# First tile's queries and keys in two transfers, and products of zeros on TensorE ahead of the first tile: a windowed-attention and mixture kernel on one core

## The chip, the core and the metric

The kernel runs on one core of a Trainium2 chip. The core has five engines with a queue each, taken in order: TensorE (PE in the profile; its weight loads are PEld), VectorE (DVE), ScalarE (ACT), GpSimd (POOL) and SyncE (SP, which issues the transfers here). They meet only at semaphores. The metric is the device time of one execution in microseconds (us); several executions are timed, and their median counts.

## The reference

There are 8 batches, 8 heads, 576 positions and 64 numbers per head. Each position attends to itself and the 63 before it. The result, 4608 tokens of 512 numbers, goes through a dense layer of 1024 with a softmax-weighted activation and a layer norm, and through a second dense layer back to 512.

```python
rel = pos[:, None] - pos[None, :]
mask = (rel >= 0) & (rel < window)            # window = 64
scores = np.where(mask, scale * (q @ k.T), -1e9)
attn = exp(scores - max) / (sum + 1e-9)
x = attn @ v                                   # tokens x 512
...
h = x @ w_in                                   # 512 -> 1024
solu = h * softmax(h)
ln = (solu - mean) / sqrt(var + 1e-6) * g_ln
y = ln @ w_out                                 # 1024 -> 512
```

## The kernel before, in words

The 4608 tokens are cut into 36 tiles of 128 (two windows of 64). Per tile t the work runs through these steps; the names are those of the rows further down.

- `load`: one transfer brings the tile's queries and keys, `qk` (640 KB, 128 partitions by 1280 numbers, for four pairs of heads), a second one the values `v`. SP issues them.
- `scores` (L356): 16 products of 64x128 on PE into `pS`, in two plan steps x = 0 and 1 of eight products (two pairs of heads each). `pS` has one buffer, of two banks of the accumulation memory; the even heads lie in one, the odd heads in the other.
- `softmax`: eight masked row maxima on DVE (L371, a custom instruction and a read of its result `nmx`), eight exponentials on ACT (L376), the sums' reciprocals (`rec`, L389 and L392, DVE) and eight scalings (L394, on DVE for tile 0, on POOL for the others).
- `transposes` (L410, PE into `t`, copied out as `PT` by L415) and `values` (L434, PE into `pX`, copied out as `xH` by L444).
- `moe_in` (into `pH`, one buffer): plain products for tiles 0 to 2 (L466), for the later ones three passes of split operands (L477). `moe_norm`: row maximum on DVE (L492), exponential on ACT (L494), product with the row on DVE (L497, the last reader of `pH`), square sum (L503) and small steps.
- `moe_transpose` (L534) and `moe_out` (into `pO`: L559 for tile 0, L571 later) follow two tiles behind.

The weights come as 64-bit numbers in eight blocks: `w_0` to `w_3` of the first matrix, `w_4` to `w_7` of the second; `w_0` comes in two halves. Each block is turned into 32-bit numbers by one step on ACT (L278) and four on DVE, L280, L282, L284 and L286, which must follow each other. All of that falls into the first 62 us.

The order in each engine's queue is not the order of the code. `Plan` collects every step as an operation with an engine, a cost and the tiles that it reads and writes; `Plan.order` then lists them with its own clock: whichever operation can begin first by the listed costs goes next, and among those ready the one that is due first. PE's and SP's operations keep the program's order among themselves, except those marked `loose` (here `scores`, `transposes` and `values` of tile 0), which go when they are ready. A transfer is ready, by the plan's cost, 2600 ns after its issue. What is written into the queue in this order is then run strictly in it.

Of the kernel before, what the change touches and what calls it, by code (L numbers as in the profile page):

```python
# [11 lines left out]
BF16 = mybir.dt.bfloat16  # L12
# [5 lines left out]
P = 128  # L18
WIN = 64
# [138 lines left out]
def tile_window_attention_solu_moe(  # L158
# [17 lines left out]
    nc = tc.nc  # L176

    NT, DM = out.shape
    w_in, w_out = w_in.bitcast(I32), w_out.bitcast(I32)
    DFF = w_in.shape[1] // 2  # L180
    NPAIR = DM // P
# [8 lines left out]
    const = ctx.enter_context(tc.tile_pool(name="const", bufs=1))  # L190
# [6 lines left out]
    ps_o = ctx.enter_context(tc.tile_pool(name="ps_o", bufs=1, space=bass.MemoryType.PSUM))  # L197
# [15 lines left out]
    for first in (0, None, 1):  # L213
        t = masks[first] = const.tile([P, P], F32, name=f"mask{first}")
        nc.gpsimd.tensor_copy(t[:WIN], band[:WIN, :P])
        nc.gpsimd.tensor_copy(t[WIN:], band[WIN:, WIN:])
        if first is not None:
            nc.gpsimd.memset(t[first * WIN:(first + 1) * WIN, :WIN], NEG)

    w_inH = const.tile([P, NC, DFF], F32R, name="w_inH")  # L220
    w_outH = const.tile([P, NF, DM], F32R, name="w_outH")
    g_sb = const.tile([P, NF], F32, name="g_sb")
# [3 lines left out]
    plan = Plan(RINGS)  # L226

    def T(tag, n, shape, dtype=F32, pool=None):

        if (tag, n) not in plan.tiles:  # L230
            plan.tiles[tag, n] = (pool or sb).tile(
                shape, dtype, tag=tag, name=f"{tag}_{n}", bufs=RINGS[tag])
        return plan.tiles[tag, n]

    def first_of(t):

        return {0: 0, NBLK - 1: 1}.get(2 * t % NBLK)
# [56 lines left out]
    def prep(i):  # L294
        if i < NC:
            weight_block(i, w_in[i * P:(i + 1) * P, :].rearrange("p (a n) -> p a n", a=2), None)
        else:
            f = 2 * (i - NC)
            weight_block(i, w_out[f * P:(f + 2) * P, :].rearrange("(a p) n -> p a n", p=P),
                         lambda x: g_sb[:, f + x:f + x + 1])  # L300
# [10 lines left out]


    def QK(t):
        return T("qk", t, [P, NPAIR * (2 * P + WIN)])

    def Q(t):
        return QK(t)[:, :NPAIR * P].rearrange("d (p s) -> d p s", p=NPAIR)

    def K(t):
        return QK(t)[:, NPAIR * P:].rearrange("d (p s) -> d p s", p=NPAIR)  # L320

    def V(t, half):
        return T("v", t, [P, 2, DM])[:, half]
# [1 line left out]
    def load(t, parts=range(2)):  # L325

        if 0 in parts:
            plan.dma(P * P * 40, lambda: nc.sync.dma_start(QK(t), qk[t]), [], [("qk", t)])


        if 1 in parts:
            plan.dma(P * P * 32, lambda: nc.sync.dma_start(
                T("v", t, [P, 2, DM]).rearrange("p a n -> p (a n)"), v[t]), [], [("v", t)])

    def SS(t):
        return T("sS", t, [P, H, P])

    def PS(t):
        return T("pS", t, [P, 2, NPAIR, P], pool=ps_s)

    def scores(t):
        first = first_of(t)

        def emit(ps=range(NPAIR)):
            q, k = Q(t), K(t)

            for p in ps:
                for half in range(2):
                    for r in range(2):
                        rs = slice(r * D, (r + 1) * D)  # L350
                        keys = k[rs, p, half * WIN:half * WIN + P]
                        if first == half:
                            a = k[rs, p, (half + 1) * WIN:(half + 2) * WIN]
                            keys = bass.AP(
                                tensor=a.tensor, offset=a.offset, ap=[a.ap[0], [0, 2], a.ap[1]])
                        nc.tensor.matmul(  # L356
                            PS(t)[half * WIN:(half + 1) * WIN, r, p],
                            q[rs, p, half * WIN:(half + 1) * WIN], keys, start=True, stop=True)

        for x in range(2):  # L360
            plan.op("PE", 500, lambda x=x: emit((2 * x, 2 * x + 1)), [("qk", t)], [("pS", t, x)],
                    loose=t < LOOSE)

    def softmax(t):
        def cols(tag, h):
            return T(tag, t, [P, H], pool=st)[:, h:h + 1]

        mk = masks[first_of(t)]
        for h in range(H):

            plan.op("DVE", 215, lambda h=h: nc.vector.tensor_tensor_reduce(  # L371
                SS(t)[:, h], PS(t)[:, h % 2, h // 2], mk, scale=-SCALE, scalar=BIG,
                op0=ALU.add, op1=ALU.min, accum_out=cols("nmx", h)),
                [("pS", t, h // 4)], [("sS", t, h), ("nmx", t, h)], lat=300)
        for h in range(H):
            plan.op("ACT", 390, lambda h=h: nc.scalar.activation(  # L376
                SS(t)[:, h], SS(t)[:, h], AF.Exp, bias=cols("nmx", h), scale=-1.0,
                accum_out=cols("sm", h)),
                [("nmx", t, h)], [("sS", t, h), ("sm", t, h)], lat=400)

        def rec():
            return T("rec", t, [P, H], pool=st)

        engine, v, cost = ("POOL", nc.gpsimd, 360) if t else ("DVE", nc.vector, 200)
        n = H if t else H // 2
        for o in range(0, H, n):
            s = slice(o, o + n)
            R = ("rec", t, o)
            plan.op("DVE", 160, lambda s=s: nc.vector.tensor_scalar_add(  # L389
                rec()[:, s], T("sm", t, [P, H], pool=st)[:, s], 1e-9),  # L390
                [("sm", t, h) for h in range(o, o + n)], [R])
            plan.op("DVE", 160, lambda s=s: nc.vector.reciprocal(rec()[:, s], rec()[:, s]), [], [R])  # L392
            for h in range(o, o + n):
                plan.op(engine, cost, lambda h=h: v.tensor_scalar(  # L394
                    SS(t)[:, h], SS(t)[:, h], rec()[:, h:h + 1], 0.0, ALU.mult, ALU.add),
                    [R], [("sS", t, h)])
# [152 lines left out]
    def moe_out(t, middle=None):  # L549
# [25 lines left out]
        def ot():  # L575
            return T("ot", t, [P, DM])

        plan.op("ACT", 580, lambda: nc.scalar.copy(ot(), PO()), [tag], [("ot", t)])
        plan.dma(P * DM * 4, lambda: nc.sync.dma_start(out[t * P:(t + 1) * P, :], ot()), [("ot", t)], [])

    def on(f, t, *args):
        if 0 <= t < NTILE:
            f(t, *args)


    load(0, range(1))
    prep(0)
    scores(0)
    softmax(0)
    load(0, range(1, 2))  # L590
    prep(1)
    prep(2)
    load(1)
    transposes(0)
    values(0)
    scores(1)
    softmax(1)
    prep(3)
# [6 lines left out]
    prep(7)  # L605
    for t in range(NTILE + BEHIND):
        on(load, t + AHEAD + 1)
        if t == PLAIN_IN:
            for i in range(NC):
                split(i)  # L610
        on(moe_in, t, 0)
        if t == 0:
            scores(2)
            softmax(2)
# [70 lines left out]
```

## Time and profile before

| | |
|---|---|
| timed runs before | median 587.1 us of 3 (587.02 to 589.51) |
| the profiled execution, its own time | 586.37 us |
| its span, first to last instruction | 584.6 us |
| PE busy | 561.5 us, 96% of the span |
| DVE, ACT, POOL busy | 54%, 55%, 31% of the span |
| SP's transfers | 60.30 MB on one queue |

The span is shorter than the execution's own time by 1.8 us, which lie around it. PE is the busiest engine by far, but in the first tenth of the span, where the weights are turned into 32-bit numbers, DVE and ACT are the busy ones; later shares of one engine say nothing on that stretch.

### The profile page before, as it was taken

What the parts mean: (1) busy time and instruction counts of PE and PEld (TensorE: products, weight loads), DVE (VectorE), ACT (ScalarE), POOL (GpSimd) and SP (SyncE); (2) the same over time, 40 slices, a digit from 0 to 9 for tenths busy, and PEclk for the clock granted to TensorE, in tenths of its full rate; (3) what the DMA queues carried; (4) which work ended last, traced back from release to release, by engine and by line L of the source; (5) the groups of instructions that cost most, each with busy time, mean ns of one, the idle gap of its engine ahead of it and who ended that gap; (6) DMA issues with size and microseconds to landing.
All of it is one profiled execution on the core that took longest, in us unless ns stands there. A gap on an engine that the chain in (4) does not pass through costs nothing.

```text
span 584.6 us, 12281 instructions
## 1 busy us (share of the span) xinstructions
PE 561.5 (96%) x4576; PEld 449.3 (77%) x4576; DVE 316.5 (54%) x1171; ACT 320.7 (55%) x939; POOL 178.5 (31%) x406
## 2 busy tenths in 40 slices
PE   2788999999999999999999999999999999999997
PEld 2344688888888888888888888888888888888875
DVE  4879975555555554444455444555555555554330
ACT  4579975555555555555555555555555555553331
POOL 2034445322222333333333333333223222223110
PEclk9999999999999999999999999999999999999999
DMA  8972222222223223332222322322222222300001
GB/s 331 410 286 81 98 84 88 91 87 91 100 100 100 100 100 100 100 99 94 78 92 100 100 100 100 101 100 100 96 84 87 90 83 97 100 20 19 18 19 54
DMA packets 17562, 61.07 MB, mean 104 GB/s; under 512 B 2016, under 2 KB 2016, under 8 KB 17120
## 3 DMA queue, kind: packets, MB, share of 16 engines
q1 hardware_dynamic: 17504, 60.30, 29.5%
q8 instruction: 36, 0.59, 0.4%
q14 instruction: 22, 0.18, 0.1%
HBM read 50.86 MB, written 9.44 MB: 103 GB/s over the span
## 4 chain that ended last, share of the span: by engine, by line
PE 91%; DVE 4%; ACT 3%; DMA 1%; issue 0%; ACTq 0%; DVEq 0%
PE pO L571 34%; PE pH L477 32%; PE pX L434 6%; PE pS L356 6%; PE t L534 5%; PE t L410 5%; ACT sS L376 1%; PE pO L559 1%; DVE w L284 1%; PE pX L571 1%; PE pH L466 1%; DMA qk<-qk 1%; DVE w L280 1%; ACT w L278 1%; DVE mst L492 1%; DVE w L282 0%
## 5 line engine op out<-in xcount | busy, mean ns | idle before, releaser
L394 POOL TENSOR_SCALAR sS<-sS,rec 128x128 f32<-128x128 f32 x280 | 100.0, 379 | 340.8 <-DVE rec L392 325.1
L376 ACT ACTIVATE sS<-sS,nmx 128x128 f32<-128x128 f32 x288 | 112.3, 393 | 45.2 <-DVE nmx L371 45.2
L571 PE MATMUL pO<-w_outH,yH 128*128 128x512 f32 x272 | 111.6, 410 | 0.2 <-ACT yH L543 0.2
L571 PE MATMUL pO<-w,yH 128*128 128x512 f32 x272 | 108.0, 397 | 0.0
L477 PE MATMUL pH<-w_inH,xH 128*128 128x512 f32 x264 | 107.7, 408 | 0.0
L571 PE MATMUL pO<-w_outH,yL 128*128 128x512 f32 x272 | 107.0, 393 | 0.1
L477 PE MATMUL pH<-w_inH,xL 128*128 128x512 f32 x264 | 103.7, 393 | 0.0
L477 PE MATMUL pH<-w,xH 128*128 128x512 f32 x264 | 103.4, 395 | 0.0
L543 ACT CAST yH<-t 128x512 fp32r<-128x512 f32 x70 | 37.5, 588 | 103.4 <-PE t L534 103.4
L492 DVE TENSOR_REDUCE mst<-pH 128x1 f32<-128x1024 f32 x36 | 44.1, 1225 | 72.7 <-PE pH L477 70.7
L415 ACT COPY PT<-t 128x512 f32<-128x512 f32 x39 | 22.7, 587 | 83.4 <-PE t L410 83.4
L571 PEld LDWEIGHTS pO<-w_outH,yH 128*128 128x128 f32 x272 | 51.0, 187 | 17.1 <-issue 5.0
L571 PEld LDWEIGHTS pO<-w_outH,yL 128*128 128x128 f32 x272 | 51.1, 188 | 13.2 <-DVE yL L545 0.5
L514 POOL TENSOR_SCALAR e<-e,mst 128x512 f32<-128x512 f32 x72 | 55.5, 777 | 18.8 <-PE t L410 11.3
L477 PEld LDWEIGHTS pH<-w_inH,xL 128*128 128x128 f32 x264 | 49.6, 188 | 12.3 <-issue 0.2
L371 DVE CUSTOM_DVE_ANT_0 sS<-pS,maskNone 128x128 f32<-128x128 f32 x224 | 51.5, 286 | 13.9 <-PE pS L356 13.9
L571 PEld LDWEIGHTS pO<-w,yH 128*128 128x128 f32 x272 | 51.1, 188 | 10.2
L477 PEld LDWEIGHTS pH<-w_inH,xH 128*128 128x128 f32 x264 | 49.6, 188 | 10.9 <-DVE mst L502 0.2
L477 PEld LDWEIGHTS pH<-w,xH 128*128 128x128 f32 x264 | 49.7, 188 | 10.0
L376 ACT ACTIVATION_READ_ACCUMULATOR sS<-sS,nmx 128x1 f32 x288 | 54.3, 188 | 0.0
L545 DVE TENSOR_TENSOR yL<-t,yH 128x512 fp32r<-128x512 f32 x70 | 44.8, 681 | 4.9 <-ACT yH L543 4.9
L356 PE MATMUL pS<-qk 64*64 64x128 f32 x1152 | 41.5, 284 | 5.8 <-DMA qk<-qk 4.8
(69 smaller groups left out, 726.4 us busy)
## 6 DMA issues: line engine op xcount, KB each, us to landing
qk<-qk SPq DMA_DIRECT2D x36, 640.0 KB, 4.2
v<-vS SPq DMA_DIRECT2D x36, 512.0 KB, 3.3
y<-ot SPq DMA_DIRECT2D x36, 256.0 KB, 2.2
raw<-w_out SPq DMA_DIRECT2D x4, 1024.0 KB, 9.3
raw<-w_in SPq DMA_DIRECT2D x3, 1024.0 KB, 11.9
raw<-w_in SPq DMA_DIRECT2D x2, 512.0 KB, 6.5
g_sb<-gT SPq DMA_DIRECT2D x1, 4.0 KB, 13.5
```

Source lines behind the costliest of these rows:

```text
L356: nc.tensor.matmul(PS(t)[half * WIN:(half + 1) * WIN, r, p], q[rs, p, half * WIN:(half + 1) * WIN], keys, start=True, stop=True)
L371: plan.op("DVE", 215, lambda h=h: nc.vector.tensor_tensor_reduce(SS(t)[:, h], PS(t)[:, h % 2, h // 2], mk, scale=-SCALE, scalar=BIG, op0=A ...
L376: plan.op("ACT", 390, lambda h=h: nc.scalar.activation(SS(t)[:, h], SS(t)[:, h], AF.Exp, bias=cols("nmx", h), scale=-1.0, accum_out=cols(" ...
L394: plan.op(engine, cost, lambda h=h: v.tensor_scalar(SS(t)[:, h], SS(t)[:, h], rec()[:, h:h + 1], 0.0, ALU.mult, ALU.add), [R], [("sS", t, h)])
L410: nc.tensor.transpose(pA()[:, i], SS(t)[:, 4 * x + i], ident)
L434: nc.tensor.matmul(PX(t)[r * D:(r + 1) * D, p, ks], V(t, half)[:, h * D:(h + 1) * D], PT(t)[:, h, ks], start=True, stop=True)
L477: plan.op("PE", 233, lambda n=n, c=c, x=x, w=w: nc.tensor.matmul(PH(t)[:, hs], x(t)[:, c], WH(c, h) if w is WH else WL(c)[:, h], start=(n ...
L492: plan.op("DVE", 1150, lambda: nc.vector.tensor_reduce(nmax(), PH(t), axis=AX.X, op=ALU.max, negate=True), [("pH", t)], [key(0)])
L514: plan.op("POOL", 770, lambda h=h, hs=hs: nc.gpsimd.tensor_scalar(E(t)[:, hs], E(t)[:, hs], nmean(), kk(), ALU.add, ALU.mult), [key(4), ke ...
L543: plan.op("ACT", 560, lambda hs=hs, pT=pT: nc.scalar.copy(YH(t)[:, hs], pT()), [("t", n)], [("yH", t, h)])
L545: plan.op("DVE", 620, lambda hs=hs, pT=pT: nc.vector.tensor_sub(YL(t)[:, hs], pT(), YH(t)[:, hs].bitcast(F32)), [("t", n), ("yH", t, h)], ...
L571: plan.op("PE", 233, lambda f=f, i=i, x=x, k=k, y=y, w=w: nc.tensor.matmul(PO(), y(t)[:, f], w(i, x), start=(f == k == 0), stop=(f == NF - ...
```

## The change: what it does

The first tile's `qk` comes in two transfers of 320 KB, one for the first two pairs of heads and one for the other two; for that the host lays the tile out as two halves, each with its queries and keys. `Q` and `K` now return one pair of heads. `scores` of step x waits for half x alone. `zeros` is a constant of 128x512 in bf16, filled by DVE. `turn` puts products of zeros on PE, 128x128 by 128x512, into a buffer of `pO` that nothing reads: eight in the code ahead of the first weight block, twelve behind the first softmax. They are not `loose`.

```diff
+    zeros = const.tile([P, 512], BF16, name="zeros")
+    nc.vector.memset(zeros, 0.0)
...
     def QK(t):
-        return T("qk", t, [P, NPAIR * (2 * P + WIN)])
...
+        return T("qk", t, [P, 2, NPAIR // 2 * (2 * P + WIN)])
+
+    def Q(t, p):
+        o = p % 2 * P
+        return QK(t)[:, p // 2, o:o + P]
+
+    def K(t, p):
+        o = 2 * P + p % 2 * (P + WIN)
+        return QK(t)[:, p // 2, o:o + P + WIN]
...
-            plan.dma(P * P * 40, lambda: nc.sync.dma_start(QK(t), qk[t]), [], [("qk", t)])
+            for x in (0, 1) if t == 0 else (slice(0, 2),):
+                plan.dma(P * P * (20 if t == 0 else 40), lambda x=x: nc.sync.dma_start(QK(t)[:, x], qk[t][:, x]),
+                         [], [("qk", t, x)] if t == 0 else [("qk", t, 0), ("qk", t, 1)])
...
-            plan.op("PE", 500, lambda x=x: emit((2 * x, 2 * x + 1)), [("qk", t)], [("pS", t, x)],
+            plan.op("PE", 500, lambda x=x: emit((2 * x, 2 * x + 1)), [("qk", t, x)], [("pS", t, x)],
                     loose=t < LOOSE)
...
+    def turn(n, count):
+        for _ in range(count):
+            plan.op("PE", 215, lambda: nc.tensor.matmul(
+                T("pO", n, [P, DM], pool=ps_o), zeros[:, :P], zeros, start=True, stop=True), [], [("pO", n)])
...
     load(0, range(1))
+    turn(-1, 8)
     prep(0)
     scores(0)
     softmax(0)
+    turn(-1, 12)
     load(0, range(1, 2))
```

Where the planner puts them is read from the queues. PE's queue before, at the program's start; the words in brackets are the semaphores that an instruction waits for, `DMAHW` those of transfers:

```order
L681 UNCONDITIONAL_BRANCH [waits barrier_Pool_Activation_PE_DVE_SP_release]
L356 MATMUL pS_0_115<-qk_0_110 64x128 [waits DMAHW0_49]
L356 MATMUL pS_0_115<-qk_0_110 64x128 x15
L410 MATMUL t_0_170<-ident_79,sS_0_134 128x128 [waits DVE_49,Pool_49]
L410 MATMUL t_0_170<-ident_79,sS_0_134 128x128 [waits DVE_49] x3
```

The same place in the changed kernel (its lines are some ten further down: L366 is L356 of before, L420 is L410, L593 the product of zeros). The first two rows stand eighteen times, one pair after the other, ahead of the rest:

```order
L593 LDWEIGHTS zeros_103
L593 MATMUL pO_-1_112<-zeros_103 128x512
L366 MATMUL pS_0_137<-qk_0_114 64x128 [waits DMAHW0_49]
L366 MATMUL pS_0_137<-qk_0_114 64x128 x7
L593 LDWEIGHTS zeros_103
L593 MATMUL pO_-1_112<-zeros_103 128x512
L593 LDWEIGHTS zeros_103
L593 MATMUL pO_-1_112<-zeros_103 128x512
L366 MATMUL pS_0_137<-qk_0_114 64x128 [waits DMAHW1_49,DVE_49]
L366 MATMUL pS_0_137<-qk_0_114 64x128 x7
L420 MATMUL t_0_192<-ident_79,sS_0_147 128x128 [waits DVE_49,Pool_49]
```

So eighteen of the twenty products come before the first scores, and the second half of the scores waits for DVE as well: the count that it waits for is reached when the row maxima of the first two heads (one in each bank of `pS`) are done. The third row maximum in turn waits for that second half.

DVE's queue before, where the last scalings of tile 0 (L394) and the weight block `w_1` meet:

```order
L286 SCALAR_TENSOR_TENSOR w_0_151<-raw_0_112,w_0_151 128x512
L394 TENSOR_SCALAR sS_0_134<-sS_0_134,rec_0_153 128x128
L280 TENSOR_SCALAR w_1_193<-w_1_193 128x1024
L394 TENSOR_SCALAR sS_0_134<-sS_0_134,rec_0_153 128x128
L282 TENSOR_SCALAR w_1_193<-w_1_193 128x1024
L394 TENSOR_SCALAR sS_0_134<-sS_0_134,rec_0_153 128x128
L284 SCALAR_TENSOR_TENSOR w_1_193<-raw_1_145,w_1_193 128x1024
L394 TENSOR_SCALAR sS_0_134<-sS_0_134,rec_0_153 128x128
L280 TENSOR_SCALAR w_2_205<-w_2_205 128x1024
L286 SCALAR_TENSOR_TENSOR w_1_193<-raw_1_145,w_1_193 128x1024
```

And in the changed kernel:

```order
L290 SCALAR_TENSOR_TENSOR w_0_175<-raw_0_125,w_0_175 128x512
L404 TENSOR_SCALAR sS_0_147<-sS_0_147,rec_0_177 128x128 x4
L284 TENSOR_SCALAR w_1_219<-w_1_219 128x1024
L286 TENSOR_SCALAR w_1_219<-w_1_219 128x1024
L288 SCALAR_TENSOR_TENSOR w_1_219<-raw_1_173,w_1_219 128x1024
L290 SCALAR_TENSOR_TENSOR w_1_219<-raw_1_173,w_1_219 128x1024
L284 TENSOR_SCALAR w_2_246<-w_2_246 128x1024
```

The four scalings now stand together ahead of the block, and the four steps of `w_1` follow each other with nothing between.

The third place is on DVE too, behind the products of tile 1 into `pH` (L492 is the row maximum over them, L497 their last reader, L371 the row maxima of tile 4's scores). Before:

```order
L280 TENSOR_SCALAR w_5_454<-w_5_454 128x1024
L492 TENSOR_REDUCE mst_1_475<-pH_1_414 128x1
L511 TENSOR_TENSOR mst_0_313<-mst_0_313 128x1
L282 TENSOR_SCALAR w_5_454<-w_5_454 128x1024
L371 ISA sS_4_520,nmx_4_521<-pS_4_485,mask1_99 128x128
...
L497 ISA e_1_508,mst_1_475<-pH_1_414,e_1_508 128x1024
L497 ISA mst_1_475 128x1
L371 ISA sS_4_520,nmx_4_521<-pS_4_485,mask1_99 128x128
...
L284 SCALAR_TENSOR_TENSOR w_5_454<-raw_5_287,w_5_454 128x1024
```

Five row maxima stand ahead of L497 there, three and L284 of `w_5` behind it. In the changed kernel:

```order
L284 TENSOR_SCALAR w_5_477<-w_5_477 128x1024
L286 TENSOR_SCALAR w_5_477<-w_5_477 128x1024
L502 TENSOR_REDUCE mst_1_509<-pH_1_439 128x1
L521 TENSOR_TENSOR mst_0_337<-mst_0_337 128x1
L381 ISA sS_4_535,nmx_4_536<-pS_4_511,mask1_99 128x128
...
L288 SCALAR_TENSOR_TENSOR w_5_477<-raw_5_313,w_5_477 128x1024
L507 ISA e_1_551,mst_1_509<-pH_1_439,e_1_551 128x1024
L507 ISA mst_1_509 128x1
```

All eight row maxima and L284 of `w_5` (here L288) now stand ahead of the last reader of `pH` (here L507). Apart from the rows above, and the second half of tile 0's `pX`, which moves ahead of tile 1's scores, PE's queue is unchanged.

## Rows read from the trace of the kernel before

**Rows 1.** The page: the TensorE clock granted in 40 slices, and the last chain by engine.
```profile
PEclk9999999999999999999999999999999999999999
...
PE 91%; DVE 4%; ACT 3%; DMA 1%; issue 0%; ACTq 0%; DVEq 0%
```
**Rows 2.** Busy time by stretch: start:end and length, busy us by engine, clock, DMA share, GB/s.
```profile
15.00:23.00 8.00, 6.00 (x40) 3.12 (x39) 7.71 (x15) 2.31 (x5) 0.00 (x0) 1.00 1.02 412
54.00:62.00 8.00, 7.04 (x87) 4.71 (x86) 8.00 (x10) 8.00 (x16) 0.00 (x0) 1.00 0.06 18
300.00:315.26 15.26, 15.26 (x130) 12.57 (x129) 7.83 (x31) 8.27 (x25) 4.83 (x12) 1.00 0.32 102
```
**Rows 3.** Order of time on PE: start, us, line, tiles, count, idle before and its releaser.
```profile
4.78 1.98 PE L356 MATMUL pS<-qk 64*64 64x128 f32 x32 [4.78 <-DMA qk<-qk]
...
12.51 1.12 PE L434 MATMUL pX<-PT,v 128*64 128x64 f32 x16 [0.68 <-ACT PT L415]
...
18.60 1.98 PE L356 MATMUL pS<-qk 64*64 64x128 f32 x32
20.51 2.57 PE L466 MATMUL pH<-w,xH 128*128 128x512 f32 x4
23.01 0.69 PE L434 MATMUL pX<-PT,v 128*64 128x64 f32 x16
...
31.57 1.10 PE L356 MATMUL pS<-qk 64*64 64x128 f32 x32
...
37.72 7.13 PE L466 MATMUL pH<-w,xH 128*128 128x512 f32 x16 [0.84 <-ACT xH L444]
...
49.26 7.10 PE L466 MATMUL pH<-w,xH 128*128 128x512 f32 x16 [1.42 <-DVE mst L497]
...
58.83 0.63 PE L534 MATMUL t<-ident,e 128*128 128x128 f32 x4 [0.21 <-DVE PT L415]
```
**Rows 4.** Chain that ended last, in order of time: start, us, what.
```profile
0.73 4.00 DMA qk<-qk
...
61.57 7.07 PE pO L559 x16
68.63 2.80 PE pH L477 x12
```
**Rows 5.** Order of time on SP and POOL at the start.
```profile
0.73 0.38 SPq L328 DMA_DIRECT2D qk<-qk  x1
0.87 0.26 POOL L205 MEMSET band<- 128x192 f32 x1
```
**Rows 6.** Order of time on DVE, 6 to 32 us.
```profile
6.95 0.29 DVE L371 CUSTOM_DVE_ANT_0 sS<-pS,mask 128x128 f32<-128x128 f32 x1 [6.95 <-PE pS L356]
...
8.44 0.28 DVE L371 CUSTOM_DVE_ANT_0 sS<-pS,mask 128x128 f32<-128x128 f32 x1
...
9.51 0.43 DVE L280 TENSOR_SCALAR w<-w 128x512 f32<-128x512 f32 x1 [0.38 <-ACT w L278]
...
15.12 0.69 DVE L280 TENSOR_SCALAR w<-w 128x1024 f32<-128x1024 f32 x1 [0.40 <-ACT w L278]
...
25.58 0.69 DVE L280 TENSOR_SCALAR w<-w 128x1024 f32<-128x1024 f32 x1 [1.10 <-ACT w L278]
...
26.40 0.69 DVE L282 TENSOR_SCALAR w<-w 128x1024 int32<-128x1024 int32 x1
27.12 1.23 DVE L284 SCALAR_TENSOR_TENSOR w<-raw,w 128x1024 int32<-128x1024 int32 x1
```
**Rows 7.** Order of time on ACT, 7 to 10 us.
```profile
7.29 0.40 ACT L376 ACTIVATE sS<-sS,nmx 128x128 f32<-128x128 f32 x1 [5.28 <-DVE nmx L371]
...
8.84 1.20 ACT L278 ACTIVATE w<-raw 128x512 f32<-128x512 f32 x2
```
**Rows 8.** Order of time on DVE, 46 to 49 us.
```profile
46.83 0.29 DVE L371 CUSTOM_DVE_ANT_0 sS<-pS,mask 128x128 f32<-128x128 f32 x1
...
47.89 1.22 DVE L497 CUSTOM_DVE_ANT_0 e<-pH,e 128x1024 f32<-128x1024 f32 x1
```

More of the change, by code (lines that the diff above doesn't have):

```diff
@@ L313, in QK @@
     def QK(t):
-        return T("qk", t, [P, NPAIR * (2 * P + WIN)])
[L316 to L320, printed above, removed]
+        return T("qk", t, [P, 2, NPAIR // 2 * (2 * P + WIN)])
[5 more added lines that the diff above has]
+        return QK(t)[:, p // 2, o:o + P + WIN]
     def V(t, half):
@@ L344, in emit @@
         def emit(ps=range(NPAIR)):
-            q, k = Q(t), K(t)
             for p in ps:
+                q, k = Q(t, p), K(t, p)
                 for half in range(2):
@@ L350, in emit @@
                         rs = slice(r * D, (r + 1) * D)
-                        keys = k[rs, p, half * WIN:half * WIN + P]
+                        keys = k[rs, half * WIN:half * WIN + P]
                         if first == half:
-                            a = k[rs, p, (half + 1) * WIN:(half + 2) * WIN]
+                            a = k[rs, (half + 1) * WIN:(half + 2) * WIN]
                             keys = bass.AP(
@@ L357, in emit @@
                             PS(t)[half * WIN:(half + 1) * WIN, r, p],
-                            q[rs, p, half * WIN:(half + 1) * WIN], keys, start=True, stop=True)
+                            q[rs, half * WIN:(half + 1) * WIN], keys, start=True, stop=True)
         for x in range(2):
-            plan.op("PE", 500, lambda x=x: emit((2 * x, 2 * x + 1)), [("qk", t)], [("pS", t, x)],
+            plan.op("PE", 500, lambda x=x: emit((2 * x, 2 * x + 1)), [("qk", t, x)], [("pS", t, x)],
                     loose=t < LOOSE)
@@ L662 @@
     qk = _np.stack([_np.concatenate([
-        qT[:, :, i:i + 2].reshape(P, -1), kT[:, :, [max(i - 1, 0), i, i + 1]].reshape(P, -1)], axis=1)
+        qT[:, :, i:i + 2].reshape(P, 2, -1), kT[:, :, [max(i - 1, 0), i, i + 1]].reshape(P, 2, -1)], axis=2)
         for i in range(0, n, 2)])
```

## The prediction

> **What bounds the kernel now.** I read the busy time by stretch first. In the middle of the run PE is busy for all of 15.26 us out of 15.26, and the chain that ended last is 91% PE [rows 1, 2]. A tile's products cannot go faster by this change, and behind tile 1's scores PE's queue is the same as before. So what the change is worth is the moment at which PE stops waiting for others: its last wait at the start ends at 58.83 [rows 3]. Behind that, every shift of PE is carried to the end unaltered: PE has no idle time to absorb it.
>
> Before that moment the limits differ. In 15 to 23 us DVE is busy 7.71 of 8 us and PE 6.00; in 54 to 62 DVE and ACT are both busy 8.00 of 8 [rows 2]. DVE turns the eight weight blocks into 32-bit numbers there, beside the first softmaxes. The reader should see that DVE is the queue to count in: a step that PE makes faster shows in the end only where DVE was idle for it.
>
> Then the order of time on PE. The same 32 records of scores take 1.98 us at 4.78 and at 18.60, and 1.10 us at 31.57; sixteen records of `pX` take 1.12 us at 12.51 and 0.69 at 23.01 [rows 3]. The granted clock stands at 1.00 in the stretch of 15 to 23 us and in all 40 slices [rows 1, 2], so that column does not show it; the durations do: PE runs at its lower level (1.2 GHz) at the start and at its upper one (2.4 GHz) later. When does it rise? The sixteen `pH` records at 37.72 take 7.13 us, 0.445 each, twice that at the lower level. The four at 20.51 stretch over 2.50 us, to 23.01: with x of them slow, 0.89x + 0.445(4 - x) = 2.50, x = 1.6. The rise came at about 20.51 + 1.6 * 0.89 = 21.9, when PE had run without a gap since 18.60, 3.3 us. The run of 1.98 us at 4.78 did not bring it.
>
> **The change, part by part.**
>
> *The zeros and their place.* DVE is idle until 6.95 [rows 6], so filling `zeros` costs it nothing, but PE waits for it. POOL's fill of 128x192 took 0.26 us [rows 5]; with the engines released at 0.73 [rows 5], PE begins at about 1.1. Eighteen products stand ahead of the first scores. No row shows a bf16 product; the nearest of 512 columns are those at 68.63, twelve in 2.80, 0.233 each at the upper level [rows 4], hence 0.467 at the lower. If the clock rises after 3.3 us of run as it did before, 3.3/0.467 = 7.1 products are slow and 10.9 * 0.233 = 2.55 us follow: the scores begin at 1.1 + 3.3 + 2.55 = 6.95, against 4.78 before. So most of the twelve products meant for the time behind the scores stand ahead of them, and delay them by 2.2 us. Bounds: upper level from the first product on, 18 * 0.233 = 4.2, start at 5.3; no rise at all, 18 * 0.467 = 8.4, start at 9.5. I take 6.95, the row that is nearest.
>
> The Trainium skill ("TensorE: Matmul & The Clock Gate", section "Wait — 56ns, not 53.3ns?") gives 215.7 ns from start to start of such products at the upper level and 426.7 at the lower. By it, an estimate, 7.7 are slow and 10.3 * 0.216 = 2.2 follow: the scores would begin 0.35 us sooner, and the sum below would be smaller by as much. No run here shows it yet.
>
> *The split transfer.* The whole transfer landed at 4.73 [rows 4]; its issue takes SP 0.38 us [rows 5], so the second half lands at about 5.1 and later transfers are issued 0.38 us later. PE asks for either half at 6.95 or after: landing sooner is worth nothing here. The later issue is hidden too: ACT began `w_0` at 8.84 straight behind its exponentials, with no wait for the transfer [rows 7], and it will get there later still. If PE asked for the first half at 4 us, the split would be worth about half of 640 KB at 412 GB/s [rows 2], 0.8 us.
>
> *The two halves of the scores.* Eight products at the upper level take 1.10/2 = 0.55 us: done at 7.5, and 0.19 us later, as from 6.76 to 6.95, the first row maximum starts at 7.7 (before 6.95). It and the second, 0.21 us apart ((8.44 - 6.95)/7), are read out 0.30 us after the second starts, at about 8.2; only then may the second half of the scores go. The two products of zeros between take 0.47 us and are hidden in that wait. The second half ends at 8.8, the third row maximum starts at 9.0 and the eighth at 9.0 + 5 * 0.21 = 10.1, against 8.44 [rows 6]. On ACT the first exponential followed the row maximum by 0.34 us and `w_0` came 1.55 us later, 0.39 for each of four [rows 7]; now the third follows at 9.35 and `w_0` at 9.35 + 0.78 = 10.1, 1.3 us later than before. DVE's first weight step, L280, waits for that: 9.51 becomes 10.8 [rows 6].
>
> *What absorbs it.* From there to the end of `w_3` DVE had two idle times of note, 0.40 us at 15.12 and 1.10 at 25.58, both for ACT's weight step [rows 6]. ACT was late because it stood behind copies of PE's slow transposes and `pX`; with PE at the upper level, `pX` takes 0.7 instead of 1.12, the scores of tile 1 1.10 instead of 1.98, and ACT reaches both steps in time. So 1.5 us come back. In their place, the steps of `w_1` now follow each other without other work between: L284 started 0.72 us after L282 at 26.40 [rows 6], where the span without waiting is 0.60, so 0.12 for each of some four pairs of steps, 0.5 us. First term: +1.3 - 1.5 + 0.5 = +0.3 us at the end of `w_3` and so at tile 0's `pH`. Its bounds go with the start of the scores: 1.65 less (-1.4) and 2.55 more, with both halves of the scores 0.45 slower each (+3.7). If PE fell back to the lower level in its pause behind the scores, tile 1's scores would end some 1.6 us later, of which DVE would feel about 0.5, within these bounds.
>
> *The last reader of `pH`, tile 1.* Here the new order costs. PE waited 1.42 us before tile 2's products at 49.26 for L497, which ran at 47.89 [rows 3, 8]. Now L282 of `w_5` moves ahead of L492: the row maxima of tile 4 still start at 46.83, but all eight, 1.7 us, go first, and then L284, 1.23 less 0.1 that overlaps, 1.13 [rows 6, 8]. L497 starts at 46.83 + 1.7 + 1.13 = 49.65, 1.76 us later, and PE's products at 51.0. Behind them PE's wait of 0.21 us at 58.83, for a copy of DVE [rows 3], can shrink; DVE, busy without a gap there [rows 2], must not come later for that. I give back 0.2. Second term: +1.6 us. Bounds: +2.0, and 0 if the delay is used up by waits that were there anyway.
>
> *Sum.* 586.37 + 0.3 + 1.6 = 588.3 for an execution like the profiled one. That one lies 0.7 us under the median of the timed runs, 587.1; against that median the sum gives 589.0, and this is the number I predict, a change of +0.3%. Some 0.5%, 2.9 us, is what a measurement of this kernel can tell from none.
>
> **The rivals.**
>
> 1. *The clock does not rise, or rises late, while the eighteen products run.* For it: the one rise seen came behind products of data, and after earlier bursts of work. Against it: nothing in the rows ties it to data. First term +3.7, sum 587.1 + 3.7 + 1.6 = 592.4. It ends over 590.0, slower, as soon as the scores begin 1 us later than I say, at 8.0.
>
> 2. *The new order behind tile 1 costs nothing,* since DVE's steps only change places and each must be done before 58.83 anyway. For it: 8.00 of 8 us busy [rows 2]. Against it: PE's wait for L497 by name [rows 3]. Then 587.1 + 0.3 = 587.4, no difference.
>
> 3. *Faster: PE's slow steps were the limit before 24 us.* In the chain of before, tile 1's scores and the first `pH` products lie end to end from 18.60 to 23.7 [rows 3]. At the upper level the scores are shorter by 0.9 us, the products by 2.50 - 4 * 0.445 = 0.7, the sixteen `pX` records of 12.51 by 0.4. If DVE gave way fully, that is -2.0, less the late start of 1.3, -0.7; with the products through at 5.3 and the start 0.4 early, -2.4. With no cost behind tile 1 the time would be 586.4 to 584.7, and under 584.2 only if more came with it. It decides itself at the scores: they must begin before 6 us. DVE's 7.71 of 8 us in that stretch [rows 2] speaks against it.
>
> **How the numbers follow.** Forecast 0.5: 588 to 590. Late or no rise 0.2, 590.0 to 592.4, slower. No cost behind tile 1 0.18, 586.5 to 588. Faster 0.12: 584.7 to 586.4 and so within 0.5%, but for 0.05 beyond. From these: slower by over 0.5% 0.20, faster 0.05, within 0.5% 0.75. The range leaves out the far half of the late rise and all of the gain below 586: 586.0 to 591.2. The likeliest case alone: 588 to 590.
>
> **What the changed profile would show.** Right: eighteen products of zeros from about 1.1 us, their spacing halving after some 3 us; scores at 7; a gap of about 0.7 us between the second and the third row maximum; `w_0` on ACT at 10; no idle time of DVE before `w_1` and `w_3`; end of tile 0's `pH` where it was, 31.6; L497 of tile 1 some 1.8 us later and tile 2's `pH` products at 51; then PE without a gap, tile after tile 15.26 us. Wrong, if scores begin before 6 or after 8, or if PE starts tile 0's `pO` products within 0.5 us of their 61.57 [rows 4].

## The result, and the profile after

The changed kernel took 592.06 us at the median (589.16 to 593.75 in eight executions), the one before 587.06 beside it (586.47 to 589.51, eight too): a ratio of 1.0067, 95% interval 1.0045 to 1.0089, slower by 0.7%. (The ratio is formed from all the executions and not from the two medians, whose quotient is 1.0085.) The profiled execution took 589.53, its span was 587.7 us: 3.16 us more than that of before, which took 586.37. The executions of the changed kernel lie in two groups, two near 589.4 and six at 591.8 to 593.8; the profiled one belongs to the first, and the second has a run of its own below.

The page first: the clock granted in 40 slices, and the shares of the last chain by engine.

```profile
PEclk8798999999999999999999999999999999999999
...
PE 93%; DVE 4%; ACT 1%; issue 0%; ACTq 0%; DVEq 0%
```

Before, the row of the clock had no digit under 9 [rows 1]. Now the first two slices do, up to 29 us, and the fourth, 44 to 59 us. The chain is PE's even more than it was.

PE in order of time, with the idle time ahead and its releaser:

```profile
1.18 5.44 PE L593 MATMUL pO_-1_112<-zeros 128*128 128x512 bf16 x18 [1.18 <-DVE zeros L222]
6.54 0.67 PE L366 MATMUL pS<-qk 64*64 64x128 f32 x16
7.14 0.60 PE L593 MATMUL pO_-1_112<-zeros 128*128 128x512 bf16 x2
7.97 0.67 PE L366 MATMUL pS<-qk 64*64 64x128 f32 x16 [0.22 <-DVE nmx L381]
11.73 1.08 PE L420 MATMUL t<-ident,sS 128*128 128x128 f32 x4 [3.09 <-DVE sS L404]
13.49 1.12 PE L444 MATMUL pX<-PT,v 128*64 128x64 f32 x16 [0.68 <-ACT PT L425]
...
18.60 1.99 PE L366 MATMUL pS<-qk 64*64 64x128 f32 x32
...
29.21 1.98 PE L476 MATMUL pH<-w,xH 128*128 128x512 f32 x4 [2.86 <-DVE w L290]
...
37.65 7.13 PE L476 MATMUL pH<-w,xH 128*128 128x512 f32 x16 [1.23 <-ACT xH L454]
...
51.25 8.80 PE L476 MATMUL pH<-w,xH 128*128 128x512 f32 x16 [3.47 <-DVE mst L507]
```

Read it against [rows 3]. The scores begin at 6.54 instead of 4.78. The products of tile 1 begin at 37.65, where they were at 37.72: the late start is made good by then. Those of tile 2 begin at 51.25 instead of 49.26, 2.0 us late, and take 8.80 us instead of 7.10. These two together are 3.7; in the chain tile 0's `pO` products come 3.23 us later than before [rows 4], so 0.5 of it comes back in the waits between. Behind 62 us PE has no wait over 0.25, and the 3.2 us reach the end as 3.16. The chain's row:

```profile
64.80 7.06 PE pO L569 x16
```

Busy time by stretch shows what happened to the clock (columns: start:end and length, busy us of PE, its weight loads, DVE, ACT, POOL, the granted clock, DMA share, GB/s):

```profile
10.00:12.00 2.00, 0.27 (x2) 0.30 (x2) 1.64 (x10) 2.00 (x8) 0.00 (x0) 0.71 1.03 434
12.00:20.00 8.00, 5.51 (x68) 4.39 (x71) 7.90 (x17) 4.58 (x10) 0.00 (x0) 0.50 1.01 419
...
50.00:52.00 2.00, 0.75 (x2) 0.54 (x3) 2.00 (x4) 2.00 (x13) 0.44 (x1) 0.95 1.02 418
52.00:55.00 3.00, 3.00 (x4) 1.04 (x4) 3.00 (x4) 2.56 (x7) 0.00 (x0) 0.50 0.04 14
```

It was raised during the products of zeros and was back at 0.50, the lower level, before the transposes of 11.73, after PE had stood idle for 3.09 us. So `pX` at 13.49 and tile 1's scores at 18.60 took 1.12 and 1.99 us as they had before [rows 3]. It fell a second time behind the idle time of 3.47 us that ends at 51.25: not in it, but some 0.5 us after the products had begun, as the 0.95 of the stretch from 50 to 52 and the 0.50 behind it show. About four of tile 2's sixteen products ran at the lower level: 1.70 us more, at 0.445 more for each.

DVE in order of time, at the start and behind tile 1:

```profile
7.40 0.29 DVE L381 CUSTOM_DVE_ANT_0 sS<-pS,mask 128x128 f32<-128x128 f32 x1 [6.28 <-PE pS L366]
...
8.71 0.29 DVE L381 CUSTOM_DVE_ANT_0 sS<-pS,mask 128x128 f32<-128x128 f32 x1 [0.79 <-PE pS L366]
...
10.50 0.43 DVE L284 TENSOR_SCALAR w<-w 128x512 f32<-128x512 f32 x1 [0.36 <-ACT w L282]
...
48.46 1.50 DVE L288 SCALAR_TENSOR_TENSOR w<-raw,w 128x1024 int32<-128x1024 int32 x1
49.88 1.21 DVE L507 CUSTOM_DVE_ANT_0 e<-pH,e 128x1024 f32<-128x1024 f32 x1
```

The weight step that stood at 9.51 [rows 6] is at 10.50; the idle times of 0.40 and 1.10 us in those rows are gone. The last reader of tile 1's `pH` starts at 49.88 instead of 47.89 [rows 8], behind eight row maxima and a weight step of 1.50 us.

### The profile page after: what moved, and what is told of

Its sections match the earlier page's. It is cut to its first block, busy times and chain, and to the rows that moved or that the text cites. A ratio compares the mean times of both kernels' runs of the same rounds, so it can differ in the third digit from the quotient of the medians.

```text
span 587.7 us, 12328 instructions
## 1 busy us (share of the span) xinstructions
PE 567.8 (97%) x4596; PEld 451.9 (77%) x4596; DVE 317.4 (54%) x1172; ACT 321.7 (55%) x939; POOL 178.0 (30%) x406
## 4 chain that ended last, share of the span: by engine, by line
PE 93%; DVE 4%; ACT 1%; issue 0%; ACTq 0%; DVEq 0%
PE pO L581 34%; PE pH L487 31%; PE pX L444 6%; PE pS L366 6%; PE t L544 5%; PE t L420 5%; PE pH L476 3%; PE pO L569 1%; DVE w L288 1%; PE pX L581 1%; PE pO_-1_112 L593 1%; DVE w L290 1%; DVE sS L381 1%; ACT sS L386 1%; DVE w L284 0%; DVE w L286 0%
## 5 line engine op out<-in xcount | busy, mean ns | idle before, releaser
L404 POOL TENSOR_SCALAR sS<-sS,rec 128x128 f32<-128x128 f32 x280 | 98.8, 375 | 348.3 <-DVE rec L402 332.7
L521 DVE TENSOR_TENSOR mst<-mst 128x1 f32<-128x1 f32 x36 | 5.8, 160 | 73.5 <-POOL mst L520 73.5
```

The lines of the kernel that those rows point to most:

```text
L404: plan.op(engine, cost, lambda h=h: v.tensor_scalar(SS(t)[:, h], SS(t)[:, h], rec()[:, h:h + 1], 0.0, ALU.mult, ALU.add), [R], [("sS", t, h)])
```

## The experiments

Every kernel below computes the whole reference; the products of zeros go into a buffer of `pO` that the first real product overwrites. Times are medians; each ratio is to executions of the kernel before on the same chip. Three chips were used, so a time is best read beside that of the kernel before on its own chip.

Two theories stood after the result. **Theory A**: the loss is made behind tile 1, by DVE's new order and by the fall of the clock that the longer wait brings, and the start is neutral. **Rival B**: it is made at the start, by the late first tile and by the clock in tile 0's zone.

**The order of before, with the eighteen products and the split.** The planner sees one transfer and no product; two transfers are issued in the one step, and the products are emitted ahead of its list.

```diff
-            plan.dma(P * P * 40, lambda: nc.sync.dma_start(QK(t), qk[t]), [], [("qk", t)])
+            def both():
+                for x in (0, 1) if t == 0 else (slice(0, 2),):
+                    nc.sync.dma_start(QK(t)[:, x], qk[t][:, x])
+            plan.dma(P * P * 40, both, [], [("qk", t)])
...
+        turn(-1, 18)
         for emit in order:
```

> Zeros and split transfer in, but every engine's order as in the kernel before: eighteen products of zeros stand at the head of PE's queue outside the plan, the first tile's transfer is one step of the plan that issues two. Theory A (the planner's new order behind tile 1, and the drop of the clock in the longer pause that it makes, cost nearly all of the 5 us): the late first scores cost at most 1 us, PE's pause before tile 2's pH products is 1.4 us again as before, their sixteen records take 7.1 us, no drop of the clock there; 587.0 to 588.3. Rival B (the products of zeros at the start cost it, by the late first tile): about 592, as the changed kernel.

Measured: 590.71 us, ratio 1.0040 (1.0024 to 1.0056). PE in order of time:

```profile
7.05 1.10 PE L368 MATMUL pS<-qk 64*64 64x128 f32 x32
...
21.91 3.76 PE L478 MATMUL pH<-w,xH 128*128 128x512 f32 x4
...
32.23 3.68 PE L478 MATMUL pH<-w,xH 128*128 128x512 f32 x4 [2.32 <-DVE w L290]
...
53.66 7.10 PE L478 MATMUL pH<-w,xH 128*128 128x512 f32 x16 [1.55 <-DVE mst L509]
```

Behind tile 1 nothing is lost: a wait of 1.55 us, as the 1.42 of [rows 3], and products of 7.10. But the start is dear. The row of before for the last four `pH` records of tile 0:

```profile
29.66 1.98 PE L466 MATMUL pH<-w,xH 128*128 128x512 f32 x4 [2.33 <-DVE w L286]
```

Here they come 2.57 us later: DVE's first weight step starts 1.40 later (10.91), and DVE's idle ahead of `w_3` grows from 1.10 to 2.26, since the first `pH` records take 3.76 us instead of 2.57 [rows 3], the clock having risen later. They are also 1.70 slower, for the clock fell again at the end of the pause of 2.32 us ahead of them. Of the 2.57 only the 1.40 can be laid on the zeros: in the kernel before with products in that later pause alone (below), the same first `pH` records take 3.78 us and DVE's idle ahead of `w_3` is 2.48. The time, 590.71, lies between what theory A (588.3 at most) and rival B (about 592) said: theory A's neutral start does not hold in this order, and rival B's full price isn't reached either.

**The new order without the products.** The planner counts them as in the changed kernel, and nothing is emitted.

```diff
-            plan.op("PE", 215, lambda: nc.tensor.matmul(
-                T("pO", n, [P, DM], pool=ps_o), zeros[:, :P], zeros, start=True, stop=True), [], [("pO", n)])
+            plan.op("PE", 215, lambda: None, [], [("pO", n)])
```

> The changed kernel's order on every engine and its split transfer, but no product of zeros is issued (the plan counts them, nothing is put on PE). Theory A: L507 of tile 1 still follows the eight row maxima and the weight step, PE pauses over 3 us before tile 2's pH products, the clock falls there and they take over 8 us; first scores start at about 4.3 at the lower level; 590 to 592. Rival B: 587 or under, since the first tile is early again.

Measured: 588.53 us, ratio 1.0016 (1.0000 to 1.0032); the profiled execution took 587.38. PE in order of time:

```profile
3.75 1.13 PE L366 MATMUL pS<-qk 64*64 64x128 f32 x16 [3.75 <-DMA qk<-qk]
5.64 1.13 PE L366 MATMUL pS<-qk 64*64 64x128 f32 x16 [0.76 <-DVE nmx L381]
...
27.34 1.98 PE L476 MATMUL pH<-w,xH 128*128 128x512 f32 x4 [2.86 <-DVE w L290]
35.79 7.13 PE L476 MATMUL pH<-w,xH 128*128 128x512 f32 x16 [1.23 <-ACT xH L454]
...
49.10 8.80 PE L476 MATMUL pH<-w,xH 128*128 128x512 f32 x16 [3.19 <-ACT sS L386]
```

The half transfer lets PE begin 1.0 us sooner than the 4.78 of [rows 3]; tile 0's last `pH` records then come at 27.34, 2.32 us before those of before. DVE's first weight step, at 8.63, is 0.88 sooner than in [rows 6], and the two idle times there, 1.50 us, are gone: together 2.38, near the 2.32. Against the changed kernel they come 1.87 us sooner, as the third row maximum does (6.84 against 8.71): here the late start is carried one for one. So the products' delay costs about 2 us, profiled execution against profiled execution 2.15. The loss behind tile 1 is here too, without any product: a wait of 3.19 us and products of 8.80. The median lies between the two forecasts, 590 to 592 and 587 or under: the loss is made at both places.

**Products of zeros in the pause behind tile 1.** Fourteen, before tile 2's products, in the changed kernel.

```diff
+    def hold(count):
+        for _ in range(count):
+            plan.op("PE", 0, lambda: nc.tensor.matmul(
+                T("pO", -1, [P, DM], pool=ps_o), zeros[:, :P], zeros, start=True, stop=True), [], [("pO", -1)])
...
+            if t == 1:
+                hold(14)
```

> The changed kernel with fourteen more products of zeros on PE in the pause between tile 2's pX and its pH products (3.0 us at the upper level), and no other order changed. Theory A: pH products of tile 2 start where they did, 51.2 to 51.4, but take 7.1 us instead of 8.8, PE starts pO at about 63.1 instead of 64.7; 587.9 for an execution like the profiled one, and in the median 588 to 589, so 3 to 4 us less than the changed kernel. Rival C (the drop of the clock costs nothing, since DVE is busy there and PE waits for DVE afterwards): 592, as the changed kernel.

Measured: 591.13 us, ratio 1.0038 (1.0015 to 1.0061); one of its eight executions, of 709.49, stands alone and stays unexplained.

```profile
50.97 2.97 PE L598 MATMUL pO_-1_112<-zeros 128*128 128x512 bf16 x13 [0.16 <-issue]
54.54 7.10 PE L476 MATMUL pH<-w,xH 128*128 128x512 f32 x16 [0.60 <-ACT sS L386]
```

With PE kept busy the same products take 7.10: the 1.70 us are the clock's, and it is the idle time that brings the fall. From the start of tile 1's products to that of tile 0's `pO` the stretch lasts 25.77 us here, 27.08 in the changed kernel and 23.78 in the kernel before: 1.3 of the 1.7 come back, and the longer wait stays. The forecast for the median, 588 to 589, was missed: 591.13 stays inside the spread of the changed kernel's. In the profiled execution the clock fell ahead of tile 0's last `pH` records too, as in the next run, and they took 3.78 us; that this holds for the other executions is not shown.

**The changed kernel once more**, for the slower of its two groups.

> The changed kernel once more, to see another of its executions: six of its eight lie near 592, the profiled one at 589.5. Theory A: an execution at 592 has the clock at the lower level for one stretch more, in tile 2's pH products (they take some 10.5 us instead of 8.8) or behind them. Rival B: it loses the time in the first 30 us.

Measured: 590.15 us, ratio 1.0044 (1.0024 to 1.0063); five executions at 589.5 to 590.2, four at 591.4 to 592.6. The profiled one took 591.38. PE, then busy time by stretch:

```profile
29.96 3.37 PE L476 MATMUL pH<-w,xH 128*128 128x512 f32 x4 [2.66 <-DVE w L290]
...
53.13 8.80 PE L476 MATMUL pH<-w,xH 128*128 128x512 f32 x16 [3.19 <-ACT sS L386]
```
```profile
28.00:30.00 2.00, 0.04 (x1) 0.04 (x1) 2.00 (x4) 0.40 (x1) 0.00 (x0) 0.84 1.02 408
30.00:32.00 2.00, 2.00 (x3) 0.96 (x4) 0.01 (x1) 0.00 (x0) 1.77 (x6) 0.50 1.01 401
```

So the place is rival B's, not theory A's: tile 2's products take 8.80 again. The slower group has a third fall of the clock, in PE's pause before the last `pH` records of tile 0, where PE has 0.04 us of work in 28 to 30: 3.37 us for four records instead of 1.98. In this execution the clock also rose later in the products of zeros, and the first scores came at 7.28 instead of 6.54. The group's mean clock is 0.985; all executions of 591 and more show that or less, all of the faster group 0.988. So the medians of the two series, 592.06 and 590.15, differ by how many executions fell there: six of eight, four of nine.

**Eight products instead of eighteen**, with the order of before, as in the first experiment.

> As the first of these runs (order of the kernel before on every engine, split transfer), but eight products of zeros at the head of PE's queue instead of eighteen. Theory A' (the ten products that run beyond the landing of the first tile cost what the first tile comes later, and nothing gives it back): products end at about 4.5, scores about 2.5 us sooner than with eighteen, and the time falls by as much, 588.2 or less against 590.7; beside the kernel before 586 to 587.5, since its scores run at the upper level. Rival D (the products cost by themselves, by the clock falling later at other places): it stays within 1 us of 590.7.

Measured: 586.25 us, ratio 0.9992 (0.9974 to 1.0010), not to be told from the kernel before. The median is 4.5 us under that of the kernel with eighteen, but on another chip, and with fewer falls of the clock: by their mean clock, 0.985 or 0.986 against 0.988 and more, four of twelve executions lost it once more here, ten of eleven there. The two profiled executions both did, and they differ by 1.80 us, the last `pH` records of tile 0 by 1.61 (30.62 against 32.23). That is nearer to the price of the ten products than 4.5. PE in an execution of 588.91:

```profile
1.18 3.59 PE L595 MATMUL pO_-1_112<-zeros 128*128 128x512 bf16 x8 [1.18 <-DVE zeros L222]
4.70 1.99 PE L368 MATMUL pS<-qk 64*64 64x128 f32 x32
```

The scores start at 4.70, at the time of the kernel before (4.78), and run at the lower level all the same: 1.99 us. So the forecast time came, but not the faster scores that it was to come with. Of the two numbers tried, eight end in time and do not raise the clock for the scores, and eighteen raise it and end late.

**The split with tile 1's last reader ahead.** No products. The planner is told by rule that L497 of tile 1 goes before ACT's and DVE's later steps there (`early` is that reader; `LATE` are the first steps of `w_6` and `w_7`, L284 of `w_5` and three row maxima).

```diff
-    turn(-1, 8)
...
-    turn(-1, 12)
...
+LATE = [("C", 6), ("C", 7), ("W", 5), ("S", 4, 5), ("S", 4, 6), ("S", 4, 7)]
...
+        early = self.named["L", 1]
+        for late in LATE:
+            before[self.named[late]].setdefault(early, False)
```

> The split transfer alone, no zeros; three rules to the planner put the last reader of tile 1's pH ahead of the last three row maxima of tile 4's scores and of the weight steps, as in the kernel before; the other changes of the order stay. Theory A': first scores at 3.75 and tile 0's pH at 29.3 as in the run without products, PE's pause before tile 2's pH products 1.4 instead of 3.2 us, no drop of the clock there, products 7.1 us; 1.8 + 1.7 us less than that run, so 585 (584.5 to 585.7), and faster than the kernel before by 2 us. Rival E (DVE's work before 59 us is the same in any order, so an earlier reader only makes other steps late): 587.4 or more, no better than the kernel before.

Measured: 585.03 us, ratio 0.9958 (0.9943 to 0.9974), faster than both kernels. The same kernel on another chip:

> The same without any product, beside it on the same chip: the split transfer alone with tile 1's last reader kept ahead. 584.5 to 585.5; if it came out above 586, the gain seen on the other chip would not hold.

Measured: 585.27 us, ratio 0.9965 (0.9948 to 0.9982). PE of the first of the two runs, and its row of DVE:

```profile
27.37 1.98 PE L485 MATMUL pH<-w,xH 128*128 128x512 f32 x4 [2.77 <-DVE w L298]
...
47.43 7.10 PE L485 MATMUL pH<-w,xH 128*128 128x512 f32 x16 [1.49 <-ACT w L303]
...
59.43 7.13 PE L579 MATMUL pO<-w,yH 128*128 128x512 f32 x16
```
```profile
46.05 1.22 DVE L516 CUSTOM_DVE_ANT_0 e<-pH,e 128x1024 f32<-128x1024 f32 x1
```

Tile 0's last `pH` records start where they did without products (27.37 against 27.34), the wait behind tile 1 is 1.49 us again, and the clock holds through 7.10. Rival E fell. What is left of the change is its split transfer and the order at the start that comes with it: 2.1 us sooner at `pO`, 0.4% in the time. In the second run's profile 1.0 us of it is lost again: ACT waited 0.72 us for the first half of `w_0` to land and PE 0.38 for tile 1's `qk`, and those `pH` records came at 28.35.

**Products in the pause before tile 0's last `pH` records**: eleven in the kernel above, nine in the kernel before, which has a second group too, at 589.

```diff
+                if t == 0 and c == NC - 1:
+                    hold(9)
```

> The run before this one, with eleven products of zeros (2.4 us at the upper level) in PE's pause of 2.9 us ahead of tile 0's last four pH records. Theory F (the executions fall into two groups, some 2.5 us apart, since the clock falls in that pause or not, by chance): all executions in the faster group, within 1 us, about 585; without the products some lie at 587.5. Rival G: the two groups stay, so they come from elsewhere.

Measured: 584.69 us, ratio 0.9953 (0.9935 to 0.9970): not to be told from 585.03. The nine executions spread over 1.7 us, from 584.15 to 585.89, and not over 1.

> The kernel before with nothing but nine products of zeros (1.9 us) in the same pause, there 2.3 us long. Theory F: its executions, of which 12 in 29 lie at 589.0 to 589.7 and 17 at 586.3 to 587.5, all lie in the lower group; median 586.8. Rival G: the two groups stay.

Measured: 586.98 us, ratio 0.9993 (0.9979 to 1.0008), and twelve executions from 586.30 to 588.13. Of the 32 executions of the kernel before beside them, eleven took 589.15 to 589.71, all with a mean clock of 0.997, and the others 586.26 to 587.51, all with 1.0. With PE kept busy in that pause the upper group is gone, as theory F said. The gain in the time is too small to be told from none, and theory F's limit of 587.5 is passed by four executions, at 587.6 to 588.1. The profiled one is among them: its clock rose later in tile 0, and the first four `pH` records took 3.78 us instead of 2.57 [rows 3]. In the split kernel there was less to lose: in its first run three of twelve executions, at 586.1 to 586.2, have a mean clock of 0.997, with the products none of nine; the later run has three such and two at 587.9, with 0.994.

```profile
20.57 3.78 PE L476 MATMUL pH<-w,xH 128*128 128x512 f32 x4
...
28.85 1.89 PE L465 MATMUL pO_-1_284<-zeros 128*128 128x512 bf16 x8
31.11 1.98 PE L476 MATMUL pH<-w,xH 128*128 128x512 f32 x4 [0.37 <-DVE w L289]
```

**Products where they delay no scores**: ten behind the second half of tile 0's scores, in the split kernel with the reader ahead.

```diff
+    hold(10)          # each step listed as reading ("pS", 0, 1), so that it follows the scores
```

> The split transfer alone, tile 1's last reader of its sums kept ahead, and ten products of zeros on TensorE behind tile 0's second half of scores, in the pause of 3.09 us that stood there before the first transposes (from 6.7 to 9.8 us): a raised clock for the whole of tile 0, without a delay of the first scores. Nothing of the computation is left out. Theory D (VectorE, busy without a gap from 8.6 to 27.3 us in the run without the products, is the queue of that zone): the transposes, the values and tile 1's scores take half as long (0.55 instead of 1.1 us, 1.1 instead of 1.98), but the weights of tile 0's last products come when they came; tile 0's last four records start at 27.4 plus or minus 0.4, and the time is 584.5 to 585.6. Rival P (TensorE's slow steps were the limit there, the prediction's third rival): they start 1 to 2 us earlier, and the time is 583 to 584. Rival Z (the products get in the way of the first transposes): those start after 10.2, the time is 585.6 to 587.

Measured: 585.78 us, ratio 0.9971 (0.9954 to 0.9988), beside 585.27 for the same without products. PE in an execution of 587.62:

```profile
6.66 4.13 PE L484 MATMUL pO_-1_145<-zeros 128*128 128x512 bf16 x10
10.63 0.60 PE L432 MATMUL t<-ident,sS 128*128 128x128 f32 x4
11.91 0.69 PE L456 MATMUL pX<-PT,v 128*64 128x64 f32 x16 [0.67 <-ACT PT L437]
14.22 1.12 PE L432 MATMUL t<-ident,sS 128*128 128x128 f32 x4 [1.62 <-DVE sS L416]
...
28.08 3.78 PE L493 MATMUL pH<-w,xH 128*128 128x512 f32 x4 [2.70 <-DVE w L301]
```

Rival Z, in part: the clock rose only when the ten were nearly through, the transposes came at 10.63 instead of 9.84, ran fast, and had the clock back at the lower level at 14.22. So tile 0 was never held at the upper level, and theory D against rival P is not decided by this. What it does show is that products at this place brought no gain.

## What held of the forecast and what failed, by its own steps

The forecast was 589.0 us, the time 592.06, above the range's upper end of 591.2; the second series, with 590.15, lies inside. The sign was right, and slower by over 0.5% had been given 0.20. The profiled execution, at 589.53, lies 1.2 over the sum of 588.3 that was meant for it. That it is not more is partly luck: the sum leaves out a term of 1.70, and two errors of some 0.3 each run against it, a loss at the start that did not arrive and waits that gave back 0.5 instead of 0.2.

*The zeros.* Right in shape: start at 1.18 (1.1 said), scores at 6.54 (6.95). The size that was off is the product's: with 0.467 and 0.233 us, taken from 32-bit products, the sum was 5.85; it took 6.54 - 1.18 = 5.36. In the trace the products start 0.427 us apart at first and 0.216 behind the rise of the clock, so that seven are slow and eleven fast. The Trainium skill ("TensorE: Matmul & The Clock Gate", section "Wait — 56ns, not 53.3ns?") has 426.7 and 215.7 ns; the trace agrees. When the clock rises was less sure than said: after seven slow products here, about 3 us, after some ten in the profile of the second series, about 4.3 us (scores at 7.28), and in the run with eight not until the scores were about done.

*First term, +0.3 at tile 0's `pH`.* It measured -0.45 (29.21 against 29.66), inside its bounds. Its parts: the weight step came 0.99 later (+1.3 said), the two idle times of 1.50 us vanished as said, and the half microsecond for steps back to back came as said. In the changed kernel the fourth step of `w_1` starts 1.26 us after the third, on which it depends; in the kernel before, a step that does not depend on the long one ahead of it starts after 1.14:

```profile
17.65 1.22 DVE L288 SCALAR_TENSOR_TENSOR w<-raw,w 128x1024 int32<-128x1024 int32 x1
18.91 1.23 DVE L290 SCALAR_TENSOR_TENSOR w<-raw,w 128x1024 int32<-128x1024 int32 x1
```
```profile
18.65 1.22 DVE L286 SCALAR_TENSOR_TENSOR w<-raw,w 128x1024 int32<-128x1024 int32 x1
19.79 0.69 DVE L282 TENSOR_SCALAR w<-w 128x1024 int32<-128x1024 int32 x1
```

Four such pairs more make 0.48. What the sum missed is how much the idle times are worth: counted from start to start of DVE's steps they are 0.48 and 1.18 us, and a third one, 0.26 ahead of tile 1's first row maximum at 20.65, went with them; 0.99 + 0.48 - 1.92 is the -0.45. The 0.40 at 15.12 went because three more scalings of tile 0 now stand ahead of `w_1`. And the reason given for the 1.10 was wrong. PE was not at its upper level in that zone; `pX` and tile 1's scores took as long as ever. The idle of 1.10 us came from ACT's weight step of `w_3`, which before stood behind a copy of the second half of `pX`:

```profile
23.75 0.37 ACT L444 COPY xH<-pX 128x256 f32<-128x256 f32 x1 [2.27 <-PE pX L434]
...
24.41 1.14 ACT L278 ACTIVATE w<-raw 128x1024 f32<-128x1024 f32 x1
```

and in the changed kernel:

```profile
18.71 0.37 ACT L454 COPY xH<-pX 128x256 f32<-128x256 f32 x1 [0.17 <-PE pX L444]
...
23.55 1.13 ACT L282 ACTIVATE w<-raw 128x1024 f32<-128x1024 f32 x1
```

The new order puts that half ahead of tile 1's scores, the copy comes 5 us sooner, and ACT's step is no longer behind it. The runs of the new order without products have no such idle either, and those with the order of before keep it: 2.26 us in the first experiment.

*The split, "worth nothing here".* True only beside eighteen products, which hide it. Without them it brings 2.3 us at tile 0's `pH`, 0.9 by the earlier start and the rest, by DVE's rows, by the new order; no run has the split alone in the order of before, which would show either by itself. And it is the split that makes the planner choose that order: in the split kernel, which has no products in its plan, DVE's and ACT's queues run as in the changed kernel up to tile 1's last reader, where the rule begins. The change's parts were costed in one sum, and the one that gains was hidden by the one that costs.

*Second term, +1.6 behind tile 1.* The mechanism was right, and the wait is a little longer than said: L507 1.99 us later (1.76 said), tile 2's products 1.99 later (51.0 said, 51.25 measured). **The step that failed is what follows from it**: "then PE without a gap". A wait of 1.42 us that becomes 3.47 is no longer only a wait; the clock falls behind it, and the 16 products there take 1.70 us more. No term of the sum had this. The Trainium skill has such a rule ("TensorE: Matmul & The Clock Gate", section "HAM oscillation — how this bites in real kernels"): a wait between two groups of products lets the clock fall, and the second group starts slow. The rows at 51.25 agree, but for the first half microsecond, which was still fast. The prediction named a fall of the clock in a pause and priced it behind the scores alone, where DVE hides it. With this term the sum comes out: 1.99 and 1.70, less the 0.5 that comes back in later waits, are the 3.16 measured. Nothing of the 0.45 at the start adds to that; by tile 1's products it is 0.07.

*The median.* To add the sum to 586.37, and 0.7 for the median, took the group of the profiled execution for the kernel. A second group, some 2.4 us higher, holds 11 of 32 executions of before but six of eight of the changed kernel. So the medians lie 5.0 us apart: 3.16 for the profiled ones, less the 0.7, and 2.5 from 589.53 up to 592.06. Shown are the fall in the pause and its price; why it comes in more executions of the changed kernel is open. The pause's length does not settle it: the clock fell behind 2.32 and 2.66 us, and held behind 2.33 (in the kernel before), 2.77 and 2.86.

*The rivals.* The first gave nearly the right time, 592.4, by a mechanism that did not occur in the profiled execution: the clock rose in time. In the profile of the second series it rose later, and the scores came at 7.28, short of the 8.0 that the rival asked for. The second, an order without cost behind tile 1, fell: 1.8 to 2.0 us later, and the clock besides. The third, a gain of PE's faster steps in tile 0, was not put to a fair test, since the clock was never up between 14 and 18 us; the gain that exists came by the split and its order, with the clock at its lower level.

## What to carry to other kernels

Work that only keeps TensorE busy must not delay what it is to speed up: the products were counted by the planner's cost at the upper level, the first seven ran at the lower, and what they delayed was carried one for one; the eight that ended in time sped up nothing. When a change lengthens a wait of TensorE, ask what clock it comes back at: here 2.0 us more of wait cost 1.7 more in the products behind. And run the parts of a change alone: the half of this one that was called worthless is a gain of 0.4%, once the one place of its new order that costs, behind tile 1, is put back.

## What the runs showed of the hardware that was not expected

In these traces the granted clock reads 1.00 up to its first fall, whatever the level: in the kernel before it does so from the start, though records at 4.78 and 18.60 took 1.98 us and the same at 31.57 took 1.10 [rows 3]. Durations, not this column, tell the level until a digit under 9 appears.

Two groups of executions some 2.4 us apart, which looked like noise, go with one fall of the clock in one pause: nine products of zeros in that pause (eight of them in the records, 1.89 us) took the upper group of the kernel before away, none of twelve executions against 11 of 32. No execution of that upper group was profiled; the fall itself is seen in the same pause of the first experiment, in the same order.

The moment at which the clock rises in tile 0 varies too, between executions whose queue is the same up to there: the first four `pH` records took 2.57 us in the profile of the kernel before, and 3.78 in its run with products in the later pause only.
